# The token mixing's residual: by transposes of the DMA queue and adds of VectorE in PSUM, in place of matmuls with the identity

## The chip, the cores and the metric

The kernel runs on one core of one Trainium2 chip. The metric is device time in microseconds (us); a run of the kernel is one execution, and the time of a kernel is the median of its runs. The profile is of one execution.

## The reference, cut to what matters

Three blocks follow each other for each of 4 batches of 576 tokens: an attention that keeps only scores near the row's maximum, an MLP mixer (token mixing, then channel mixing, both with a residual), and a gated feed-forward with a convolution of three taps over the tokens. The change lies in the token mixing, whose result with its residual is `u`.

```python
# attention, per head
scores = where(scores >= max(scores) - tau, scores, -1e9); attn = softmax(scores); x = attn @ v
# mixer
h  = maximum(xt @ w_tok1, 0) @ w_tok2          # xt: x with channels ahead of tokens, 576 -> 256 -> 576
u  = x + h.transpose(0, 2, 1)                  # the residual in question
x2 = u + maximum(u @ w_ch1, 0) @ w_ch2         # 512 -> 1536 -> 512
# gated feed-forward
f  = maximum(x2 @ w_in, 0); gate = sigmoid(conv3(f)); out = (f * gate) @ w_out
```

## The kernel before, in words

Every large product is made of three float16 products: each operand is split into a high part and a low part (`_h`, `_l`), and high*high, high*low and low*high are added in one PSUM tile.

**Attention.** `attention(b)` walks through 36 slots of a batch: four pairs of heads, nine slots each. A slot has 128 queries: scores on PE (L308 or L312), row maximum on DVE (L324), exponential on ACT (L336), masking on DVE (L343), the split into two halves on ACT (L348) and POOL (L352), a transpose by the DMA queue of SP (L357, `pt<-ph`, nine blocks of 128x128), and some slots later the product with V on PE (L367, L370). `norm` divides by the row sum and splits the result x into `xp`: `xh` on ACT (L395), `xl` on POOL (L396), with tokens on the partitions: four blocks of 128 tokens, and a fifth with the last 64 tokens.

**Token mixing.** `tok(b, p)` runs once for each pair of heads p of each batch b. Its first step makes the hidden layer (L407) and splits it into `rh`, `rl`. Its two further steps make `u` for one stretch of tokens each (256 and 320, `SPL`): matmuls with `w_tok2` (L422) accumulate in one PSUM bank `up`, and between them PE adds the residual to the same bank: for each block of 128 tokens and for `xh` and `xl` one matmul that has the block as its weights and the identity (scaled by 1/`UDS`) as its moving operand (L427), which transposes the block and adds it. Then ACT writes the high part of `u` from the bank (L429), DVE the low part from the bank and the high part (L430), and the bank is free.

**Dense stages.** `dense(b)` follows for the whole batch: L547 (512 to 1536), L565 (1536 to 512), L598 with the convolution and the gate (`gate`: L581 on ACT, L583 twice on DVE, L585 on ACT, L586 on DVE, L587 on ACT, L588 on POOL, for each of eight row blocks f) and L621/L624 (the output product, which needs the gates of all f).

**What sets the order.** The attention of batch b+1, and its `tok`, is woven into `dense(b)` by counting steps. So the token mixing of batch 2 runs beside `dense(1)`, and that of batch 3 beside `dense(2)`: in each the first two pairs of heads fall into the stages of L565 and early L598, the third into the middle of the gates, the fourth behind the output product, right ahead of the next `dense`. A scheduler sets the final order of each engine from priorities and its own estimate of times; on the chip each engine then goes through its list strictly in order.

**Banks.** PSUM has eight banks. While attention and dense work run together, four are held by scores (two slots), one by the product with V, and three (4, 5, 6) go round between the dense tiles and `tok` (`dbank`, `free`): a bank is handed out in the order in which banks came free in the program, and PE waits if its last reader has not finished. In `dense(3)` banks 0 to 3 join them. All buffers with the tag "x" (the attention's tiles, the gate's `ct`, loads) come from one pool of 15.

Of the kernel before, what the change touches and what calls it, by code (L numbers as in the profile page):

```python
# [9 lines left out]
F16 = mybir.dt.float16  # L10
I32 = mybir.dt.int32
U16 = mybir.dt.uint16
AF = mybir.ActivationFunctionType
ALU = mybir.AluOpType
# [5 lines left out]
def kernel(ctx: ExitStack, tc: tile.TileContext, q, k, v, tau,  # L20
# [7 lines left out]
    nc = tc.nc  # L28
    B, NPR, _, S = q.shape
    H, D = 2 * NPR, 64  # L30
    P = 128
# [7 lines left out]
    NS = S // P  # L39
    R0 = NS * P  # L40
    SPL = [(0, 256), (256, S - 256)]
    NB32 = 2
# [10 lines left out]
    UDS = 1.0 / (WS * WS2)  # L53
# [6 lines left out]
    qk2 = ctx.enter_context(tc.tile_pool(name="qk2", bufs=2))  # L60
# [5 lines left out]
    V, A, G, T = nc.vector, nc.scalar, nc.gpsimd, nc.tensor  # L66
# [23 lines left out]
    for x, (sc, left) in enumerate(((0.125, 1.0), (QK, ESC))):  # L90
        V.tensor_scalar(out=qsc[:, x:x + 1], in0=tau_t, scalar1=0.0, scalar2=sc, op0=ALU.is_ge, op1=ALU.mult)
        V.scalar_tensor_tensor(out=mtaus[:, x:x + 1], in0=tau_t, scalar=-1.0 / left, in1=every,
                               op0=ALU.mult, op1=ALU.min)
# [198 lines left out]
    def dbank():  # L292

        x = free.pop(0)
        return x
# [102 lines left out]
    def tok(b, p):  # L398

        u, xp = u_t[b % 2][p], pair[b, p]["xp"]  # L400
        bk = dbank()
        rp = ps[:, bk]
        for t in range(NT):
            o = t * P
            for i, (wx, xx) in enumerate(((0, 0), (1, 0), (0, 1))):
                for j in range(NS + 1):
                    T.matmul(rp[:, o:o + P], wt1[wx][:, j, o:o + P], xp[xx][:, j],  # L407
                             start=(i == 0 and j == 0), stop=(i == 2 and j == NS))
        rh = p2.tile([P, NT, P], F16, tag="rh", name="rh")
        rl = p2.tile([P, NT, P], F16, tag="rl", name="rl")  # L410
        r3 = rp[:, :TK].rearrange("p (t c) -> p t c", t=NT)
        A.activation(out=rh, in_=r3, func=AF.Relu)
        V.scalar_tensor_tensor(out=rl, in0=r3, scalar=0.0, in1=rh, op0=ALU.max, op1=ALU.subtract)
        free.append(bk)
        yield
        rr = (rh, rl)
        for s0, n in SPL:
            bk = dbank()
            up = ps[:, bk]
            for i, (rx, wx) in enumerate(((0, 0), (1, 0), (0, 1))):  # L420
                for t in range(NT):
                    T.matmul(up[:, :n], rr[rx][:, t], wt2[wx][:, t, s0:s0 + n],  # L422
                             start=(i == 0 and t == 0), stop=(i == 2 and t == NT - 1))
                for j in range(NS + 1):
                    if i < 2 and s0 <= j * P < s0 + n:
                        m = P if j < NS else S - R0
                        T.matmul(up[:, j * P - s0:j * P - s0 + m], xp[i][:, j], ident if j < NS else ident2,  # L427
                                 start=False, stop=False)
            A.activation(out=u[0][:, s0:s0 + n], in_=up[:, :n], func=AF.Copy, scale=UDS)  # L429
            V.scalar_tensor_tensor(out=u[1][:, s0:s0 + n], in0=up[:, :n], scalar=UDS,  # L430
                                   in1=u[0][:, s0:s0 + n], op0=ALU.mult, op1=ALU.subtract)
            free.append(bk)
            if s0 == 0:
                yield
        del pair[b, p]
        yield
# [14 lines left out]
    def attention(b):  # L451
# [9 lines left out]
        for i in range(c0, c1, NSL):  # L461
            bb, p, _ = where(i + NSL)
            if bb < B:
                start(i - 1, prep(bb, p), (1, 2, 2, 1, 1, 1))
            start(i + NSL - 1 + lag + 2, tok(b, where(i)[1]), (2, 1, 1))
# [194 lines left out]
    for b in range(B):  # L660
        att = attention(b + 1) if b + 1 < B else iter(())
        n = 0
# [65 lines left out]
```

## Time and profile before

| what | value |
|---|---|
| time, three runs | 793.1, 795.9, 797.14 us; median 795.9 us |
| the profiled execution | 798.93 us, of which 797.1 us are the span from its first to its last instruction |
| PE busy | 742.8 us, 93% of the span |
| DVE, ACT, POOL busy | 495.5, 471.0, 421.8 us |
| matmuls with the identity (L427) | 160, of which 80 in batches 2 and 3 |

Busy time is the union of an engine's instructions. A matmul's duration in the profile runs from its start to the modelled end of its results, so two that follow each other overlap; what a matmul costs in a dense stream is the distance from start to start. "Idle before, releaser" says how long an engine stood idle and whose end let it go on.

### The profile page before, as it was taken

The numbers are of one execution on the slowest core, as the hardware profiler recorded it, in microseconds if no ns is written. First come the engines' busy times: TensorE is split into PE (matmuls) and PEld (weight loads), VectorE is DVE, ScalarE is ACT, GpSimd is POOL, SyncE is SP. The second block draws the span as 40 slices with busy tenths as digits, with TensorE's granted clock in tenths as the row PEclk, the third lists the DMA queues.
The fourth block names the chain that finished last, engine by engine and source line by source line (L and its number), as shares of the span: only waits on it lengthen the run. The fifth ranks groups of instructions, "written<-read, shape, count | busy, mean of one in ns | idle before, by whom it ended". The sixth has DMA issues, their size and how long they took to land. (4 is left out here: it accounts for less than half of the span.)

```text
span 797.1 us, 18473 instructions
## 1 busy us (share of the span) xinstructions
PE 742.8 (93%) x7388; PEld 562.1 (71%) x7388; DVE 495.5 (62%) x837; ACT 471.0 (59%) x998; POOL 421.8 (53%) x471
## 2 busy tenths in 40 slices
PE   5579979898998889999999999999999999999998
PEld 3457657676776675678878875788887856887764
DVE  5568877786767683367677892566876960322370
ACT  6768876775766674466566862566565751220371
POOL 5977788877687572155555771265664840000040
PEclk9889989999999999999999999999999999999999
DMA  9989998888789640368676531667664401000001
GB/s 280 195 186 173 166 240 198 187 226 192 200 219 198 106 76 28 93 135 164 135 164 131 117 54 40 139 134 156 143 133 80 76 18 58 1 1 1 2 1 60
DMA packets 195047, 97.84 MB, mean 123 GB/s; under 512 B 174096, under 2 KB 176656, under 8 KB 194960
## 3 DMA queue, kind: packets, MB, share of 16 engines
q1 hardware_dynamic: 194640, 96.39, 55.0%
q8 instruction: 58, 0.95, 0.5%
q10 hardware_dynamic: 320, 0.26, 0.1%
q14 instruction: 29, 0.24, 0.1%
HBM read 42.36 MB, written 4.72 MB: 59 GB/s over the span
## 5 line engine op out<-in xcount | busy, mean ns | idle before, releaser
L352 POOL TENSOR_TENSOR ph<-e,ph 128x576 f16<-128x576 f32 x108 | 141.2, 1308 | 98.0 <-ACT ph L348 93.0
L565 PE MATMUL ps<-act_t,wc_h 128*128 128x256 f16 (+1 forms) x768 | 148.8, 286 | 0.0
L324 DVE TENSOR_REDUCE nm<-ps 128x1 f32<-128x576 f32 x144 | 108.3, 753 | 54.2 <-PE ps L312 27.0
L308 PE MATMUL ps<-kt,qt 128*128 128x288 f32 (+1 forms) x320 | 95.1, 458 | 27.5 <-DVE act_t L343 12.1
L588 POOL TENSOR_TENSOR act_t<-ct,act_t 128x576 f16<-128x576 f32 x32 | 46.6, 1455 | 138.8 <-ACT act_t L587 135.9
L547 PE MATMUL ps<-u_h,wc_h 128*128 128x256 f16 (+1 forms) x384 | 110.0, 287 | 2.0 <-DVE act_t L522 2.0
L547 PE MATMUL ps<-u_h,wc_l 128*128 128x256 f16 (+1 forms) x384 | 109.9, 287 | 0.0
L565 PE MATMUL ps<-act_t,wc_l 128*128 128x256 f16 (+1 forms) x384 | 109.7, 286 | 0.0
L547 PE MATMUL ps<-u_l,wc_h 128*128 128x256 f16 (+1 forms) x384 | 109.4, 287 | 0.0
L343 DVE SCALAR_TENSOR_TENSOR e<-ps,thr,e 128x576 f32<-128x576 f32 x108 | 87.7, 812 | 22.3 <-ACT e L336 9.8
L547 PEld LDWEIGHTS <-wc_h 128*128 128x128 f16 x768 | 75.4, 98 | 20.3 <-issue 1.3
L565 PEld LDWEIGHTS <-wc_h 128*128 128x128 f16 x768 | 75.0, 98 | 18.9 <-issue 0.5
L308 PEld LDWEIGHTS ps<-kt,qt 128*128 128x128 f32 (+1 forms) x320 | 54.1, 197 | 46.2 <-DVE act_t L343 16.5
L367 PE MATMUL ps<-vh,pt 128*128 128x65 f16 (+1 forms) x1080 | 72.1, 195 | 7.4 <-DMA pt<-ph 7.2
L621 PE MATMUL ps<-wo_h,act_t 128*128 128x512 f16 x256 | 76.3, 379 | 1.8 <-DVE u_l L430 1.3
L583 DVE SCALAR_TENSOR_TENSOR ct<-h,cw,ct 128x576 f32<-128x576 f32 x64 | 68.3, 1068 | 15.2 <-ACT ct L581 14.6
L598 PE MATMUL ps<-u_h,wi_h 128*128 128x256 f16 (+1 forms) x256 | 73.0, 286 | 4.3 <-DVE u_l L430 3.2
L367 PEld LDWEIGHTS <-pt 128*128 128x128 f16 (+1 forms) x1080 | 62.7, 101 | 19.3 <-DMA pt<-ph 10.7
L348 ACT ACTIVATE ph<-e 128x576 f16<-128x576 f32 x108 | 73.0, 676 | 2.1 <-DVE e L343 2.1
L598 PE MATMUL ps<-u_h,wi_l 128*128 128x256 f16 (+1 forms) x256 | 73.0, 286 | 0.0
L598 PE MATMUL ps<-u_l,wi_h 128*128 128x256 f16 (+1 forms) x256 | 73.0, 286 | 0.0
L621 PEld LDWEIGHTS <-act_t 128*128 128x128 f16 x384 | 36.7, 98 | 44.0 <-issue 2.1
(113 smaller groups left out, 1621.3 us busy)
## 6 DMA issues: line engine op xcount, KB each, us to landing
st<-in_moe_w_ch_dram SPq DMA_DIRECT2D x24, 512.0 KB, 4.2
ld<-in_v_dram SPq DMA_DIRECT2D x32, 288.0 KB, 3.4
kt<-ks SPq DMA_DIRECT2D x32, 144.0 KB, 2.7
st<-in_moe_w_in_dram SPq DMA_DIRECT2D x8, 512.0 KB, 4.2
st<-in_moe_w_out_dram SPq DMA_DIRECT2D x8, 512.0 KB, 5.2
out_dram<-ot SPq DMA_DIRECT2D x16, 256.0 KB, 2.0
qt<-in_q_dram SPq DMA_DIRECT2D x8, 288.0 KB, 3.9
kt<-in_k_dram SPq DMA_DIRECT2D x16, 144.0 KB, 3.8
```

The costliest lines, as they stand in the source:

```text
L308: T.matmul(s3[o:o + m, a], f32(st["qt"])[:, q0:q0 + m], f32(st["kt"][hh])[:, a * hn:(a + 1) * hn], start=True, stop=True)
L324: crit["max"] = V.tensor_reduce(out=nm, in_=c["s3"], axis=AX.XY, op=ALU.max, negate=True)
L343: crit["mask"] = V.scalar_tensor_tensor(out=e3, in0=c["s3"], scalar=c["thr"], in1=e3, op0=ALU.is_ge, op1=ALU.mult)
L348: A.activation(out=c["ph"][:, 0:S], in_=c["e"], func=AF.Copy)
L352: G.tensor_tensor(out=c["ph"][:, S:], in0=c["e"], in1=c["ph"][:, 0:S], op=ALU.subtract)
L367: T.matmul(dst[o:o + m], pt[:, j, o:o + m], vh[:, hh, j, 0:D + 1], start=(j == 0), stop=(j == NSL - 1))
L547: T.matmul(t, wc1[wx][:, f, c], u[c][ux][:, sl], start=(c == 0 and i == 0), stop=(c == NC - 1 and i == 2))
L565: T.matmul(t, wc2[wx][:, c, f], r_t(f, rx)[:, sl], start=(by_dve(c) and f == 0 and i == 0), stop=(f == NF - 1 and i == 2))
L583: V.scalar_tensor_tensor(out=ct, in0=ht[:, kk:kk + S], scalar=cw[:, kk, f:f + 1], in1=ct, op0=ALU.mult, op1=ALU.add)
L588: G.tensor_tensor(out=g_t(f, 1), in0=ct, in1=g_t(f, 0), op=ALU.subtract)
L598: T.matmul(t, wi[wx][:, f, c], u[c][ux][:, s0:s0 + n], start=(c == 0 and i == 0), stop=(c == NC - 1 and i == 2))
L621: T.matmul(t, g_t(f, gx)[:, j * P:(j + 1) * P], wo[wx][:, f], **lim)
```

## The change

For batches 2 and 3 (`b >= NB32`) the residual of the 512 first tokens no longer goes through PE. At the start of `tok` a tile `xt` is taken from the "x" pool, POOL clears its last 64 columns, and SP's queue issues two transposes (high and low half, four blocks of 128x128 each). PE leaves out the matmuls with the identity except those of the last 64 tokens. Once PE has finished a stretch, DVE scales the bank, adds the transposed high half and writes the sum back to the bank, then adds the low half in the bank. ACT and DVE then split it as before, without the scale. Batches 0 and 1 are as before.

```diff
     def tok(b, p):
         u, xp = u_t[b % 2][p], pair[b, p]["xp"]
+        xt = None
+        if b >= NB32:
+
+            xt = qk2.tile([P, 2, S], F16, tag="x", name="xt", bufs=15)
+            G.memset(xt[:, :, R0:S], 0.0)
+            for i in range(2):
+                nc.sync.dma_start_transpose(out=xt[:, i, 0:R0].rearrange("p (j t) -> p j t", t=P),
+                                            in_=xp[i][:, 0:NS].rearrange("p j c -> p (j c)"))
         bk = dbank()
...
                 for j in range(NS + 1):
-                    if i < 2 and s0 <= j * P < s0 + n:
+                    if i < 2 and s0 <= j * P < s0 + n and (j == NS or xt is None):
                         m = P if j < NS else S - R0
                         T.matmul(up[:, j * P - s0:j * P - s0 + m], xp[i][:, j], ident if j < NS else ident2,
                                  start=False, stop=False)
-            A.activation(out=u[0][:, s0:s0 + n], in_=up[:, :n], func=AF.Copy, scale=UDS)
-            V.scalar_tensor_tensor(out=u[1][:, s0:s0 + n], in0=up[:, :n], scalar=UDS,
-                                   in1=u[0][:, s0:s0 + n], op0=ALU.mult, op1=ALU.subtract)
+            sl, up = slice(s0, s0 + n), up[:, :n]
+            if xt is not None:
+                V.scalar_tensor_tensor(out=up, in0=up, scalar=UDS, in1=xt[:, 0, sl], op0=ALU.mult, op1=ALU.add)
+                V.tensor_tensor(out=up, in0=up, in1=xt[:, 1, sl], op=ALU.add)
+            uds = UDS if xt is None else 1.0
+            A.activation(out=u[0][:, sl], in_=up, func=AF.Copy, scale=uds)
+            V.scalar_tensor_tensor(out=u[1][:, sl], in0=up, scalar=uds, in1=u[0][:, sl],
+                                   op0=ALU.mult, op1=ALU.subtract)
             free.append(bk)
```

In the new file L407 is the transposes, L430 the matmuls with `w_tok2`, L435 the matmuls with the identity, L439 and L440 the two adds, L442 and L443 the split; the lines behind `tok` are 13 further down (L583 is L596, L586 is L599).

PE's list in the fourth pair of batch 3, the stretch of 256 tokens, before:

```order
L422 LDWEIGHTS rh
L422 MATMUL ps<-wt_h,rh 128x256
L427 LDWEIGHTS xh
L427 MATMUL ps<-ident,xh 128x128
L427 LDWEIGHTS xh
L427 MATMUL ps<-ident,xh 128x128
L422 LDWEIGHTS rl
L422 MATMUL ps<-wt_h,rl 128x256
```

The same place of the new program:

```order
L430 LDWEIGHTS rh
L430 MATMUL ps<-wt_h,rh 128x256
L430 LDWEIGHTS rl
L430 MATMUL ps<-wt_h,rl 128x256
L430 LDWEIGHTS rl
L430 MATMUL ps<-wt_h,rl 128x256
```

The two matmuls of `xh` between the products of `rh` and `rl` are gone, as are the two of `xl` behind those of `rl`.

DVE's list in the third pair of batch 3, in the middle of the gates (`ct` is the gate's tile, `u_2_l` the low part of the third pair's u), before:

```order
L586 SCALAR_TENSOR_TENSOR ct<-ct,h_147 128x576
L583 SCALAR_TENSOR_TENSOR ct<-h_148,cw,ct 128x576
L430 SCALAR_TENSOR_TENSOR u_2_l<-ps,u_2_h 128x256
L583 SCALAR_TENSOR_TENSOR ct<-h_148,cw,ct 128x576
L383 TENSOR_SCALAR rc<-ps 128x5
L384 RECIPROCAL rc<-rc 128x5
L387 TENSOR_TENSOR x_9357<-ps,rc 128x4x64
L390 SCALAR_TENSOR_TENSOR x_9357<-ps,rc,blk 128x128
L583 SCALAR_TENSOR_TENSOR ct<-h_147,cw,ct 128x576
L586 SCALAR_TENSOR_TENSOR ct<-ct,h_148 128x576
L430 SCALAR_TENSOR_TENSOR u_2_l<-ps,u_2_h 128x320
L583 SCALAR_TENSOR_TENSOR ct<-h_147,cw,ct 128x576
```

The same place of the new program, up to the low part of the first stretch and a little further:

```order
L599 SCALAR_TENSOR_TENSOR ct<-ct,h_147 128x576
L439 SCALAR_TENSOR_TENSOR ps<-ps,xt 128x256
L440 TENSOR_TENSOR ps<-ps,xt 128x256
L596 SCALAR_TENSOR_TENSOR ct<-h_148,cw,ct 128x576
L443 SCALAR_TENSOR_TENSOR u_2_l<-ps,u_2_h 128x256
L596 SCALAR_TENSOR_TENSOR ct<-h_148,cw,ct 128x576
L383 TENSOR_SCALAR rc<-ps 128x5
L384 RECIPROCAL rc<-rc 128x5
L439 SCALAR_TENSOR_TENSOR ps<-ps,xt 128x320
L387 TENSOR_TENSOR x_9357<-ps,rc 128x4x64
L596 SCALAR_TENSOR_TENSOR ct<-h_147,cw,ct 128x576
```

The two adds of the first stretch now stand between the gates of two row blocks, ahead of the next L583 (L596). Of the second stretch, L439 stands among the steps of `norm`, L440 behind L390, and the low part two places behind the L586 (L599) of `h_148`, with an L583 (L596) between them.

## Rows read from the trace of the kernel before

**Rows 1.** The page: PE's busy time, and the clock granted in 40 slices.

```profile
PE 742.8 (93%) x7388; PEld 562.1 (71%) x7388; DVE 495.5 (62%) x837; ACT 471.0 (59%) x998; POOL 421.8 (53%) x471
...
PEclk9889989999999999999999999999999999999999
```

**Rows 2.** Busy times by stage: stretch, length, PE, PEld, DVE, ACT, POOL, clock, DMA.

```profile
437.00:484.00 47.00, 44.76 (x508) 33.96 (x506) 40.27 (x54) 34.64 (x73) 31.55 (x31) 1.00 0.39 77
484.00:503.00 19.00, 19.00 (x157) 11.32 (x156) 0.48 (x2) 3.65 (x9) 1.64 (x2) 1.00 0.20 72
503.00:609.00 106.00, 106.00 (x1182) 86.33 (x1180) 76.03 (x133) 65.48 (x144) 57.66 (x76) 1.00 0.66 136
609.00:657.00 48.00, 46.15 (x512) 34.62 (x511) 36.25 (x51) 33.60 (x70) 29.82 (x27) 1.00 0.29 51
```

**Rows 3.** Timeline of PE in the fourth pair of batch 3: start, us, instructions.

```profile
674.82 0.28 PE L427 MATMUL ps<-ident,xh 128*128 128x128 f16 x2
674.93 0.38 PE L422 MATMUL ps<-wt_h,rl 128*128 128x256 f16 x2
675.15 0.28 PE L427 MATMUL ps<-ident,xl 128*128 128x128 f16 x2
```

**Rows 4.** Groups of DVE by shape, 380 to 680: count, busy us, mean ns, idle before.

```profile
L583 DVE SCALAR_TENSOR_TENSOR ct<-h,cw,ct 128x576 f32<-128x576 f32 x32 | 36.3, 1134 | 3.8 <-ACT ct L581 3.5
...
L532 DVE TENSOR_TENSOR u_l<-us,u_h 128x320 f16<-128x320 f32 x6 | 6.7, 1122 | 0.1
...
L430 DVE SCALAR_TENSOR_TENSOR u_l<-ps,u_h 128x320 f16<-128x320 f32 x8 | 3.9, 485 | 1.5 <-ACT u_h L429 1.5
...
L430 DVE SCALAR_TENSOR_TENSOR u_l<-ps,u_h 128x256 f16<-128x256 f32 x8 | 3.3, 418 | 27.9 <-ACT u_h L429 27.9
```

**Rows 5.** The group of the whole span that writes PSUM from DVE.

```profile
L157 DVE SCALAR_TENSOR_TENSOR ps<-st,ps 128x512 int32<-128x512 int32 x42 | 29.1, 693 | 21.7 <-ACT ps L156 7.3 <-POOL ph L352 6.0 <-issue 5.3
```

**Rows 6.** Waits of PE between 380 and 680: us in total, times, longest.

```profile
PE ps L598 <- DVE u_l L430: 1.4, 1, 1.4
PE ps L598 <- ACT h L574: 1.0, 1, 1.0
...
PE ps L621 <- DVE u_l L430: 0.6, 2, 0.3
PE ps L621 <- ACT act_t L587: 0.3, 1, 0.3
PE ps L621 <- POOL act_t L588: 0.3, 1, 0.3
```

**Rows 7.** Timeline of DVE among the gates of `dense(2)`, third pair of batch 3.

```profile
638.40 1.00 DVE L586 SCALAR_TENSOR_TENSOR ct<-ct,h 128x576 f32<-128x576 f32 x1 [0.75 <-ACT ct L585]
641.09 1.00 DVE L583 SCALAR_TENSOR_TENSOR ct<-h,cw,ct 128x576 f32<-128x576 f32 x1 [1.69 <-ACT ct L581]
...
647.91 1.01 DVE L586 SCALAR_TENSOR_TENSOR ct<-ct,h 128x576 f32<-128x576 f32 x1 [0.75 <-ACT ct L585]
649.11 2.57 DVE L583 SCALAR_TENSOR_TENSOR ct<-h,cw,ct 128x576 f32<-128x576 f32 x2 [0.19 <-ACT ct L581]
652.42 0.76 DVE L586 SCALAR_TENSOR_TENSOR ct<-ct,h 128x576 f32<-128x576 f32 x1 [0.75 <-ACT ct L585]
```

**Rows 8.** SP's transposes of the attention: issue ns, and time to landing.

```profile
L357 SPq DMA_TRANSPOSE pt<-ph x108: 1242/1302/2678, 108.5 to 637.1; - x108
...
DMA to landing us min/median/max: 3.2/3.4/7.4
```

**Rows 9.** Timeline of POOL, second pair of batch 2: the low half of x.

```profile
421.20 0.67 POOL L396 TENSOR_TENSOR xl<-x,xh 128x256 f16<-128x256 f32 x1
```

**Rows 10.** Timeline of ACT, the same pair: the first evacuation of u.

```profile
432.36 0.38 ACT L429 ACTIVATE u_h<-ps 128x256 f16<-128x256 f32 x1 [0.28 <-PE ps L422]
```

**Rows 11.** Timeline of DVE at the seam to `dense(2)`, fourth pair of batch 2.

```profile
502.94 0.42 DVE L430 SCALAR_TENSOR_TENSOR u_l<-ps,u_h 128x256 f16<-128x256 f32 x1 [13.69 <-ACT u_h L429]
```

**Rows 12.** Timeline of PE there: the next use of that bank.

```profile
504.59 0.27 PE L547 MATMUL ps<-u_h,wc_h 128*128 128x256 f16 x1
```

## The prediction

> **What bounds the kernel now.** I read the page first, then the stages, then the waits of PE inside them. PE is busy for 742.8 of 797.1 us, and its granted clock is at the full level from slice 14 on [rows 1]; what it loses, it loses in the first 300 us, which the change does not touch. By stages [rows 2] PE is busy for all 106 us of 503 to 609 and all 19 us of 484 to 503, but for 44.8 of 47 us in 437 to 484 and 46.2 of 48 us in 609 to 657. These two are the stages of the gates, beside which the third pairs of batches 2 and 3 fall, and there DVE is the busiest engine after PE: 40.3 of 47 us and 36.3 of 48 us. The waits name what PE stood for: 1.4 + 0.6 us for L430 (a bank of PSUM that the token mixing still held), 1.0 us for the gate's L574, 0.3 + 0.3 us for the last gate (L587, L588) [rows 6]. So PE sets the pace nearly everywhere, and in the gates' stages DVE's list does, through banks and through the last gate. A matmul less on PE is worth its distance to the next one; an instruction more on DVE costs nothing until it makes a bank or a gate late.
>
> **What is removed.** Each `tok` loses eight matmuls of 128x128 (four blocks, two halves), so 8 x 8 = 64. Two of them start at 674.82 and the next matmul at 674.93 [rows 3]: 0.055 us each, their weight loads hidden. 64 x 0.055 = 3.5 us, or 0.44 us a pair of heads. The Trainium skill (TensorE: Matmul & The Clock Gate, Back-to-back issue gap) gives 81 ns as the sustained spacing of a 128-column matmul that has its own weight load; by it the saving would be 5.2 us. This trace shows 55 ns, and the sum goes by that.
>
> **What is added on DVE.** Two instructions a stretch. Before has none with a PSUM input, a float16 tile from SBUF and a PSUM output. Nearest below is L430, which has those inputs and writes SBUF: 418 ns for 256 columns, 485 for 320 [rows 4]; L157 does write PSUM, 693 ns for 512 [rows 5], which is where L430's two points lead (about 1.05 ns for each further column: 485 + 192 x 1.05 = 687). Above is L532, with all operands in SBUF: 1122 ns for 320 [rows 4]. I take L430: two adds cost 0.84 us for 256 columns and 0.97 us for 320, 14.5 us over the 16 stretches; at the upper end they would be up to 2.2 us a stretch. The skill (SBUF — State Buffer, Who interferes with whom) says that DVE with two SBUF inputs contends with a GpSimd instruction that reads SBUF and with at most one it doesn't. L583, which has two, averages 1134 ns for 576 columns [rows 4], twice what L430's slope leads to; the trace agrees, and the adds have one.
>
> **What is added in queues.** Sixteen transposes on SP of four blocks, against nine of the attention's, which take 1.30 us to issue and land 3.2 to 7.4 us later, 3.4 in the median [rows 8]; four blocks by that ratio issue in about 0.6 us (an estimate). They need `xl`; in the second pair of batch 2, the closest, it is done at 421.87, and the first evacuation starts at 432.36 [rows 9, 10], 10.5 us later. New on the list of SP is that they stand behind some of the attention's transposes, whose lead over their matmuls is several slots, and delay the loads behind them by 1.2 us, which nothing on PE waits for at once. I put this at 0; if a landing takes 7.4 us and SP is two transposes late, the cover is gone, and DVE stands at L439 for up to 2 us with row maxima and gates queued behind it. The memset on POOL (128 columns) and the "x" buffer that `xt` holds: 0, since POOL has 15 us or more free in each gates' stage [rows 2]; a late buffer would show as a late exponential.
>
> **What moves.** A bank is now held from PE's end over L439, L440, L442, L443 instead of over two steps: 0.84 or 0.97 us longer, plus DVE's queue.
>
> - *First, second and fourth pairs* (six). DVE has room or the next user of the bank is 1 us or more behind, so PE keeps its 0.44 us: -2.6 us. One exception is the seam to `dense(2)`: DVE ends L430 at 503.36 and the bank's next user starts at 504.59, 1.2 us later [rows 11, 12]. The new list of DVE has both stretches' adds ahead of the first low part: L439 can start where the evacuation on ACT started, 0.4 us ahead of 502.94; with 0.84, 0.97 and 0.42 us behind it, and a little for the second stretch's matmuls, the low part ends at 504.7 to 504.8. PE, with half of its 0.44 us less between the two, is there at about 504.4. +0.3 us. At the last seam the four more banks cover it.
> - *Third pairs* (two). Here PE gets nothing, since it waits for the last gate anyway [rows 6], and DVE's list decides. In batch 3 [rows 7] the new list puts the first two adds into the idle 1.69 us ahead of 641.09: free. From there I place the new list with the durations of the old one (each starting 0.08 us ahead of the end of the one before, as the rows do): both remaining adds, 0.80 us, are paid until the low part, and the following L586 starts 0.4 us later than its 647.91. The pair of L583 behind it waited 0.19 us for ACT, so the last L586 (652.42) is 0.2 us late. In batch 2 the new list moves three steps of `norm` ahead of the last gate as well, 2.3 us in all with the four adds, against about 2 us of idle gaps behind ACT that they fall into: 0.3 to 0.7, I take 0.5. Together +0.7 us.
>
> **Sum**: -2.6 + 0.3 + 0.7 = -1.6 us: from 798.9 us for the profiled execution to 797.3. Its own time is 3.0 us above the median of the three runs, 795.9; from there 794.3 us. That is 0.2% less. About 0.5% (4 us) is what a measurement of this kernel can tell from no change; its three runs lie that far apart.
>
> **The rivals.**
> - *PE-bound throughout: the adds are free.* The new list of PE puts more work between the third pairs' stretches and the next use of their banks (in batch 2, by the program's order, 29 matmuls of 320 columns in place of 12 behind the first stretch; behind the second 16 of 512 columns and 24 others in place of 6 and 12). Then all 3.5 us are kept and the 2.0 us of waits for L430 [rows 6] vanish: -5.5 us, 790.4. Against it: the idle time of DVE in the gates' stages is nearly all behind ACT within one gate, so it isn't free to be filled everywhere.
> - *The other side: DVE is the bound of the gates' stages.* If the adds cost what L532 does, or each delays a contended L583, a third pair costs up to 2 x 2.2 us on DVE, and PE, which waits for the last gate, pays it: 2 x 4.4 us less the 2.6 us of the other pairs, +6 us, 802. It decides from about 1.7 us of unhidden time a stretch of the two third pairs (4 x 1.7 - 2.6 = 4). For it: DVE's busy share there; against: L430's steady durations.
> - *The transposes are late.* A first pair's transposes follow two of the attention's closely; DVE then stands at L439 and PE's banks with it, 1 us in each of the eight pairs: +6 us, 802.
> - *The scheduler's other order* shifts PE's waits by 1 us here and there, with either sign; that is in the range of each case.
>
> **Chances.** The forecast (within 0.5%: 792 to 798): 0.55. The free adds: 0.26, nearly all of it faster by over 0.5%. DVE-bound 0.12, transposes late 0.07: slower. The range 790.3 to 799.5 takes in the free adds and the lower edge of the slower ones; the likeliest case alone is 792.5 to 797.
>
> **What would show it.** In the new profile: 80 - 64 = 16 matmuls of L435 in batches 2 and 3, and PE's busy time down by some 3.5 us; L439 and L440 near 0.42 and 0.485 us, steady beside POOL. Right if PE's waits for L443 stay near 2 us in all and those for L600 and L601 (the last gate) rise by under 1 us; the free adds if they sink towards 0; DVE-bound if those for L443, L600, L601 or L343 sum to 8 us and more. Idle time of DVE at L439 behind a DMA `xt` would show late transposes. I would be wrong above all in how much of the adds falls into DVE's gaps, which I placed by hand in one stage and only weighed in the other.

## The result, and the profile after

The changed kernel takes 804.9 us (median of four runs, 802.9 to 806.6); the kernel before, run beside it, 796.5 us (793.1 to 800.3). The ratio is 1.0104, 95% interval 1.0065 to 1.0143: about 8 us slower. The forecast was 794.3 us with a range of 790.3 to 799.5; the time lies outside.

The profiled execution took 803.7 us, with a span of 801.9 us. The part ahead of `dense(1)`, which the change doesn't touch, differs between executions (over the profiles of all runs, `dense(1)` starts between 320.9 and 333.6 us), so the two traces are compared from a fixed place: the first matmul of a dense stage. The rows of L547 (before) and L560 (after) with their first and last start, for `dense(1)` and `dense(2)`, before:

```profile
L547 PE MATMUL ps<-u_h,wc_h x96: 272/290/301, 330.8 to 376.7; 128*128 128x256 f16 x48, 128*128 128x320 f16 x48
L547 PE MATMUL ps<-u_h,wc_h x96: 272/290/301, 503.4 to 549.4; 128*128 128x256 f16 x48, 128*128 128x320 f16 x48
```

and after:

```profile
L560 PE MATMUL ps<-u_h,wc_h x96: 272/290/301, 329.1 to 375.0; 128*128 128x256 f16 x48, 128*128 128x320 f16 x48
L560 PE MATMUL ps<-u_h,wc_h x96: 270/290/300, 508.5 to 554.7; 128*128 128x256 f16 x48, 128*128 128x320 f16 x48
```

From the one to the other `dense(1)` lasted 503.4 - 330.8 = 172.6 us, now 508.5 - 329.1 = 179.4 us: +6.8 us. From there to PE's last matmul it is 290.2 us before and 289.9 us now. The whole loss lies in `dense(1)`, beside which batch 2's token mixing runs; batch 3's costs nothing on balance (beside it the removed matmuls alone give 2.0 us, and the adds alone take 1.9: E3 and E2 below). Within `dense(1)` it lies in the gates: from their first matmul to the first of the output product 40.3 us before and 49.5 us after.

The gates' stage in the new kernel (columns as in [rows 2]: stretch, sum, busy time of PE, its weight loads, DVE, ACT and POOL, granted clock, DMA share, GB/s):

```profile
437.00:484.00 47.00, 39.92 (x448) 31.00 (x445) 37.74 (x57) 33.93 (x71) 32.52 (x34) 0.93 0.47 92
```

In 437 to 484, PE is busy for 39.9 us against 44.8 [rows 2], and DVE, which should have more to do, for less as well: 37.7 against 40.3. Neither is the bound there any more. What PE waited for, from 380 to 680 (columns: engine and line, what it waited for, us in total, times, longest):

```profile
PE ps L367 <- DVE x L387: 2.4, 1, 2.4
PE ps L430 <- ACT h L587: 1.6, 1, 1.6
PE ps L611 <- ACT h L587: 1.6, 2, 1.1
PE ps L367 <- DMA pt<-ph: 1.5, 2, 1.4
PE ps L312 <- DVE e L343: 0.8, 2, 0.7
PE ps L634 <- DVE u_l L443: 0.6, 1, 0.6
PE ps L634 <- ACT h L587: 0.6, 1, 0.6
PE ps L560 <- DVE u_l L443: 0.3, 1, 0.3
```

Half of this is for the attention, and not for the token mixing's banks as in [rows 6]: L367 is the product with V, which waits for `norm` (L387) and for `pt`, the transposed probabilities, and L312 the scores. Together they are 4.7 us, where the kernel before has only

```profile
PE ps L312 <- DVE e L343: 0.6, 1, 0.6
```

These waits stand at 448 to 460 us, near the end of batch 2's attention. (The 3.8 us for L587, ACT's evacuation of the gate's `h`, come later: 2.3 us of them at 474 and 482 us, the rest in `dense(2)`. That they follow from the attention's delay is not shown.) Around the attention's waits the granted clock falls (columns: stretch, sum, busy time of PE, granted clock, DMA share, GB/s):

```profile
447.00:450.00 3.00, 1.02 (x14) 1.00 0.70 140
450.00:452.00 2.00, 1.39 (x27) 0.55 1.00 233
452.00:454.00 2.00, 2.00 (x21) 0.59 0.36 139
454.00:456.00 2.00, 2.00 (x19) 1.00 0.00 0
458.00:460.00 2.00, 0.64 (x5) 1.00 0.68 132
460.00:462.00 2.00, 2.00 (x32) 0.61 0.54 105
462.00:464.00 2.00, 2.00 (x10) 0.53 0.23 42
464.00:466.00 2.00, 2.00 (x34) 1.00 0.56 108
```

Twice PE has hardly worked and then runs for some 4 us near its lower level (1.2 GHz). Against full clock that is, as an estimate from these rows, 1.39 x 0.45 + 2 x 0.41 + 2 x 0.39 + 2 x 0.47 = 3.2 us. The waits in this stage sum to 7.1 us against 2.2 us before, 4.9 more; with the 3.2 us of the clock, less 1.8 us for the removed matmuls of four pairs, that gives 6.3 of the 6.8 us.

SP's list shows where the delay enters. Its transfers around the first pair's transposes, before (columns: start, length, engine and line, transfer, count):

```profile
394.09 0.53 SPq L248 DMA_DIRECT2D ld<-in_q_dram  x1
394.73 0.40 SPq L249 DMA_DIRECT2D ld<-in_k_dram  x1
```

and after:

```profile
389.60 2.80 SPq L357 DMA_TRANSPOSE pt<-ph  x2
392.49 1.23 SPq L407 DMA_TRANSPOSE xt<-xh  x1
393.78 1.26 SPq L407 DMA_TRANSPOSE xt<-xl  x1
395.13 0.53 SPq L248 DMA_DIRECT2D ld<-in_q_dram  x1
395.71 0.42 SPq L249 DMA_DIRECT2D ld<-in_k_dram  x1
```

The `pt` transposes ahead start 1.6 us earlier than before, and so does `dense(1)` itself (329.1 against 330.8 us). Then two `xt` hold the queue for 1.25 us each, and the load of the next heads' q starts 1.0 us later than before: 2.6 us lost in one place. At the second pair it happens again (q's load at 429.7 us against 426.8). Counted from the first matmul of `dense(1)`, the two loads are 2.7 and 4.6 us late, and the `pt` that PE waits for near 460 us (456.6 against 452.5 us) is 5.8 us late.

The scores of the heads that these loads are for are not what is held up. Behind the first pair's transposes come the batch's last heads; their `kt` has landed 12 us ahead of its first score in the kernel before and still 11 us ahead in the new one. Behind the second pair's come the first heads of batch 3. What the loads hold up is ACT, which goes through its list in order: the split of the new q (L226) waits for the load, and an exponential of the running attention (L336) stands behind the split. At the first pair, before:

```profile
397.24 0.78 ACT L226 ACTIVATE qs<-ld,qsc 128x576 f16<-128x576 f32 x1 [0.83 <-DMA ld<-in_q_dram]
397.92 0.72 ACT L336 ACTIVATE e<-ps,bias 128x576 f32<-128x576 f32 x1
```

and after:

```profile
398.27 0.78 ACT L226 ACTIVATE qs<-ld,qsc 128x576 f16<-128x576 f32 x1
398.95 0.72 ACT L336 ACTIVATE e<-ps,bias 128x576 f32<-128x576 f32 x1
```

Counted from the first matmul of `dense(1)`, the exponential starts 2.7 us later, and at the second pair 4.6 us later (433.66 against 430.78 us). ACT stood for these two loads before already, 0.83 and 2.07 us, so nothing covers a later one; the masking, `ph` and `pt` of the slot come behind the exponential.

### The profile page after: what moved, and what is told of

It is laid out like the page before. It is cut to its first block, busy times and chain, and to the rows that moved or that the text cites. A ratio compares the mean times of both kernels' runs of the same rounds, so it can differ in the third digit from the quotient of the medians.

```text
span 801.9 us, 18424 instructions
## 1 busy us (share of the span) xinstructions
PE 743.0 (93%) x7324; PEld 559.7 (70%) x7324; DVE 502.2 (63%) x869; ACT 470.7 (59%) x998; POOL 421.4 (53%) x479
## 5 line engine op out<-in xcount | busy, mean ns | idle before, releaser
L601 POOL TENSOR_TENSOR act_t<-ct,act_t 128x576 f16<-128x576 f32 x32 | 44.8, 1402 | 136.8 <-ACT act_t L600 135.3
L560 PE MATMUL ps<-u_h,wc_h 128*128 128x256 f16 (+1 forms) x384 | 109.7, 287 | 2.0 <-DVE act_t L535 1.5
L560 PE MATMUL ps<-u_h,wc_l 128*128 128x256 f16 (+1 forms) x384 | 109.6, 286 | 0.0
L560 PE MATMUL ps<-u_l,wc_h 128*128 128x256 f16 (+1 forms) x384 | 108.8, 286 | 0.0
L343 DVE SCALAR_TENSOR_TENSOR e<-ps,thr,e 128x576 f32<-128x576 f32 x108 | 87.7, 812 | 18.3 <-ACT e L336 8.8
L560 PEld LDWEIGHTS <-wc_h 128*128 128x128 f16 x768 | 75.2, 98 | 20.1 <-issue 1.1
L367 PE MATMUL ps<-vh,pt 128*128 128x65 f16 (+1 forms) x1080 | 75.0, 198 | 12.2 <-DMA pt<-ph 9.6
L308 PEld LDWEIGHTS ps<-kt,qt 128*128 128x128 f32 (+1 forms) x320 | 53.7, 196 | 45.6 <-DVE act_t L343 16.7
L367 PEld LDWEIGHTS <-pt 128*128 128x128 f16 (+1 forms) x1080 | 64.4, 103 | 22.3 <-DMA pt<-ph 14.1
L611 PE MATMUL ps<-u_h,wi_h 128*128 128x256 f16 (+1 forms) x256 | 74.7, 292 | 2.1 <-ACT h L587 1.6
L596 DVE SCALAR_TENSOR_TENSOR ct<-h,cw,ct 128x576 f32<-128x576 f32 x64 | 68.5, 1071 | 12.5 <-ACT ct L594 11.9
L535 DVE SCALAR_TENSOR_TENSOR act_t<-ps,act_t 128x256 f16<-128x256 f32 (+1 forms) x96 | 43.0, 455 | 39.0 <-ACT act_t L534 38.3
```

The source lines that it names most:

```text
L308: T.matmul(s3[o:o + m, a], f32(st["qt"])[:, q0:q0 + m], f32(st["kt"][hh])[:, a * hn:(a + 1) * hn], start=True, stop=True)
L343: crit["mask"] = V.scalar_tensor_tensor(out=e3, in0=c["s3"], scalar=c["thr"], in1=e3, op0=ALU.is_ge, op1=ALU.mult)
L367: T.matmul(dst[o:o + m], pt[:, j, o:o + m], vh[:, hh, j, 0:D + 1], start=(j == 0), stop=(j == NSL - 1))
L560: T.matmul(t, wc1[wx][:, f, c], u[c][ux][:, sl], start=(c == 0 and i == 0), stop=(c == NC - 1 and i == 2))
L596: V.scalar_tensor_tensor(out=ct, in0=ht[:, kk:kk + S], scalar=cw[:, kk, f:f + 1], in1=ct, op0=ALU.mult, op1=ALU.add)
L601: G.tensor_tensor(out=g_t(f, 1), in0=ct, in1=g_t(f, 0), op=ALU.subtract)
```

## The experiments

A table at their end holds the main ones. "`dense(1)`" is the time between the two first matmuls as above. Three profiled kernels in which PE's list in `dense(1)` is the same (the kernel before, E4 and E8) show 172.6, 172.8 and 173.0 us, so about half a microsecond can be read there from one profile where the lists are the same, which the times can't tell. The theories were A (the transposes on SP's queue), B (the adds on DVE) and C (the 64 matmuls had covered the attention's chain).

**E1, the transposes alone.** An excerpt of its difference from the changed kernel:

```diff
-                    if i < 2 and s0 <= j * P < s0 + n and (j == NS or xt is None):
+                    if i < 2 and s0 <= j * P < s0 + n:
...
-            if xt is not None:
-                V.scalar_tensor_tensor(out=up, in0=up, scalar=UDS, in1=xt[:, 0, sl], op0=ALU.mult, op1=ALU.add)
-                V.tensor_tensor(out=up, in0=up, in1=xt[:, 1, sl], op=ALU.add)
-            uds = UDS if xt is None else 1.0
+            uds = UDS
```

> The sixteen transposes into xt stay, xt is read by nobody, PE adds the whole residual as before and DVE has no adds: the output is the reference's. Theory A (the transposes are the loss: SP's queue is 2.5 us longer a pair, and with it the scores of the next heads fall behind the dense matmuls in PE's list): slower than before by 5 to 11 us, since nothing is saved on PE, with PE standing in the gates of dense(1) as in the changed kernel (its waits there 5 us or more). Theory B (the adds on DVE are the loss): within 1 us of before. Theory C (the 64 matmuls were cover for the attention's chain, and PE stands in their place): within 1 us of before.

Measured: +1.0% (interval 0.65 to 1.36), `dense(1)` 179.9 us. The transposes that nobody reads cost all that the change costs. The exponentials behind the two splits of q start 2.5 and 5.8 us later than before, counted from `dense(1)`. PE's waits from 375 to 500 us:

```profile
PE ps L367 <- DMA pt<-ph: 4.4, 3, 2.9
PE ps L367 <- DVE x L387: 2.1, 1, 2.1
PE ps L631 <- DVE u_l L440: 0.9, 1, 0.9
```

**E2, the adds alone.** An excerpt of its difference from the changed kernel (the transposes are out as well, and PE adds the whole residual):

```diff
+    zt = const.tile([P, 320], F16, name="zt")
+    G.memset(zt, 0.0)
...
-                V.scalar_tensor_tensor(out=up, in0=up, scalar=UDS, in1=xt[:, 0, sl], op0=ALU.mult, op1=ALU.add)
-                V.tensor_tensor(out=up, in0=up, in1=xt[:, 1, sl], op=ALU.add)
+                V.scalar_tensor_tensor(out=up, in0=up, scalar=UDS, in1=zt[:, :n], op0=ALU.mult, op1=ALU.add)
+                V.tensor_tensor(out=up, in0=up, in1=zt[:, :n], op=ALU.add)
```

> No transposes; PE adds the whole residual as before, and DVE's two adds a stretch add a constant tile of zeros, so the output is the reference's. Theory A: 0 to 2 us slower than before, from the third pairs. Theory B: slower by 6 us or more. Theory C: as A.

Measured: +0.73% (0.49 to 0.98), `dense(1)` 178.0 us. Theory A had 0 to 2 us and failed here: the adds alone cost nearly as much as the transposes alone, and the two together no more than one. But the waits are again the attention's (`pt` 3.8 us in all, the longest 2.9), not the gates', as DVE as the bound would show.

**E3, the removal alone** (neither adds nor transposes).

> The 64 matmuls are gone and nothing takes their place: the residual of the first 512 tokens of batches 2 and 3 is left out. Theory A and theory B: faster than before by 2.5 to 3.5 us (0.3 to 0.45%). Theory C: within 1 us of before or slower, PE waiting in the gates of dense(1).

Measured: -0.24% (-0.44 to -0.05), `dense(1)` 171.9 us, from its start to the end 2.7 us less. Theory C falls: PE's saving is real, about as priced.

**E4, the last batch alone** (`b > NB32` in place of `b >= NB32`).

> The change in the last batch alone; batch 2 is as before, and so is PE's list up to the last batch's attention. Theory A, as the traces of before and after place the loss (+6.6 us up to 484 us, -1.1 us from there to the end): as fast as before or up to 2 us faster, 0 to -0.25%. Theory B: half of the loss stays, slower by 3 to 5 us. Theory C: as A.

Measured: -0.1% (-0.35 to +0.17), `dense(1)` 172.8 us, and 289.8 us from there. As the traces said, the loss is batch 2's.

**E5 and E6, PE's list held fast.** Ahead of scores that it takes to be late, the scheduler may move dense matmuls that are ready. In the changed kernel it did: batch 2's attention has forty groups of scores (four matmuls each), and between the 22nd and the 23rd of them PE's list has 4.0 groups of twelve dense matmuls, where before it has 2.3; it pays at the end, with 2.0 between the third last and the last, where before it has 4.0. So I made a pair of kernels in which each step of `dense(1)` is queued on PE behind the scores that stand ahead of it in the text:

```diff
-                    T.matmul(s3[o:o + m, a], st["qt"][:, hh, q0:q0 + m],
+                    crit["score"] = T.matmul(s3[o:o + m, a], st["qt"][:, hh, q0:q0 + m],
...
-        for i, _ in enumerate(dense(b)):
+        for i, _ in enumerate(steps(dense(b), ("score",)) if b == 1 else dense(b)):
```

With it, scores and dense matmuls of `dense(1)` alternate in both kernels in the same way. The rule holds only these two: the places of the products with V and of the token mixing's matmuls, and the lists of ACT, DVE and POOL, may still differ. E5 is the kernel before with the rule, E6 the changed one.

> The kernel before, with one rule for PE's list: each step of dense(1) is queued on PE behind the scores that stand ahead of it in the program's text, so that no dense matmul can be moved ahead of scores that the scheduler thinks late. PE's list moves by at most 2 groups of 12 dense matmuls in dense(1) and is the same elsewhere. Theory A1 (it is PE's list that loses the time, not the queue's delay on the chip): 0 to 2 us either side of before. Theory A2 (the queue's delay on the chip): the same; this run is the base of the next.

> The changed kernel with the same rule: in dense(1) the dense matmuls and the scores then stand in PE's list exactly as in the pinned kernel before, while transposes, adds and the removal are all there. Theory A1: 0 to 3 us faster than the pinned kernel before (794 to 797), the gates of dense(1) from 49.4 back to 41 or 42 us. Theory A2: as slow as the changed kernel, 5 us or more over the pinned kernel before, with PE now standing at the scores. Theory B (DVE's added work): slower than the pinned kernel before by 4 us or more, DVE behind in the gates.

Measured: E5 +0.41% (0.17 to 0.65), `dense(1)` 173.6 us; E6 +0.76% (0.44 to 1.07), `dense(1)` 177.8 us. Between the two lie 4.2 us in `dense(1)`; without the rule it was 6.8. So the order of scores and dense matmuls took some 2.6 us of the loss, and most of it is left when that order is the same. Neither A1 nor A2 had that; both parts are there. PE's waits in E5, from 375 to 500 us:

```profile
PE ps L621 <- DVE u_l L430: 1.4, 1, 1.4
PE ps L367 <- DMA pt<-ph: 1.1, 1, 1.1
PE ps L598 <- DVE u_l L430: 0.5, 1, 0.5
```

and in E6:

```profile
PE ps L312 <- DVE e L343: 3.2, 3, 2.5
PE ps L367 <- DMA pt<-ph: 1.9, 2, 1.7
PE ps L634 <- ACT h L587: 1.1, 1, 1.1
PE ps L367 <- DVE x L390: 0.8, 1, 0.8
```

The dense matmuls no longer run ahead, and PE stands at the scores (L312) instead: the attention's chain itself is late.

**E7, adds and removal, no transposes** (E2's tile of zeros in the changed kernel).

> The changed kernel without the transposes: DVE adds a constant tile of zeros instead of xt, so the residual of the first 512 tokens of batches 2 and 3 is left out. The adds alone cost 5.8 us, the removal alone gave 1.9 us. If the adds cost by DVE's time (B): 802 or more, 3 to 6 us over before. If they cost through the order that they led the scheduler to (A1): anything from -2 to +6 us, decided by whether the gates of dense(1) take 40 to 42 us or 47 us and more in the profile.

Measured: +0.1% (-0.15 to +0.36), `dense(1)` 175.5 us, from there 2.0 us less than before. The gates took 45.6 us, between the two cases that the expectation names.

**E8, tile and memset alone** (E1 without the loop of the transposes).

> The kernel before with xt taken from the pool of 15 buffers and its last columns cleared by POOL, without transposes and adds: the output is the reference's. PE's list is the same as before. Theory that the buffer taken from the attention's pool is the loss: slower by 2 us or more. All others: within 1 us of before.

Measured: +0.1% (-0.24 to +0.42), `dense(1)` 173.0 us. The buffer from the attention's pool costs nothing.

**E9 and E10, transposes and adds apart, PE's list held fast** (E1 and E2 with the rule of E5).

> The transposes alone (xt is read by nobody, PE adds the whole residual), under the rule of the pinned kernels; PE's list in dense(1) stands as in both of them. Between the pinned pair, dense(1) up to its output product took 4.9 us longer with the change (1.8 us in the stage ahead of the gates, 3.3 us in the gates, less 0.2), and its list was the same. If the delay of SP's queue makes it: the gates 3 us and more over the pinned kernel before (44 us and more). If the adds make it: 41 to 42 us.

> The adds alone (of a constant tile of zeros, PE adds the whole residual), under the same rule. If the delay of SP's queue makes the 4.9 us: the gates of dense(1) at 41 to 42 us. If the adds make it: 44 us and more. If both are needed together: both runs at 42 to 43 us.

Measured: E9 +0.69% (0.35 to 1.03), `dense(1)` 177.9 us, 4.3 over E5. E10 +0.40% (0.1 to 0.71), `dense(1)` 174.1 us, 0.5 over E5. With scores and dense matmuls in the same order, the adds cost 0.5 us in `dense(1)`; the other 4.9 us of E2 were the order that they led the scheduler to. E2's trace shows most of it, on POOL: the two low halves of `norm` (L398) stand ahead of the last slot's `ph` (L354),

```profile
461.31 2.15 POOL L398 TENSOR_TENSOR xl<-x,xh 128x256 f16<-128x256 f32 x2
463.42 1.27 POOL L354 TENSOR_TENSOR ph<-e,ph 128x576 f16<-128x576 f32 x1
```

where the kernel before has `ph` first, as E10 has:

```profile
465.01 1.28 POOL L352 TENSOR_TENSOR ph<-e,ph 128x576 f16<-128x576 f32 x1
...
467.00 0.67 POOL L396 TENSOR_TENSOR xl<-x,xh 128x256 f16<-128x256 f32 x1
```

Counted from `dense(1)`, that `ph` ends 2.7 us later; PE waits 2.9 us for its `pt`, and the granted clock is at half for the 3.4 us behind.

The transposes delay the chip also where the order of scores and dense matmuls stands: against E5, the exponentials behind the two splits of q start 2.1 and 3.2 us later in E9, and 0.0 and 0.3 in E10. But E9's 4.3 us are not shown to be the queue's alone. Its lists of ACT, DVE and POOL stand in another order than E5's in many places (at 391.6 us ACT has the next slot's L329 ahead of an exponential that E5 has ahead of it, and which starts 1.7 us later for it); those of E10 hardly differ from E5's. PE's waits in E9, from 375 to 500 us:

```profile
PE ps L312 <- DVE e L343: 2.5, 2, 1.9
PE ps L608 <- ACT h L584: 1.7, 2, 1.6
PE ps L367 <- DMA pt<-ph: 1.4, 1, 1.4
PE ps L608 <- DVE u_l L440: 0.5, 1, 0.5
```

**E11 and E12, the change only where PE doesn't wait**: the fourth pairs alone (`b >= NB32 and p == 3`), and with them the first two pairs of the last batch.

> The change in the fourth pairs of batches 2 and 3 alone, which run beside the output products, where the attention is over and SP's queue empty. By the stages of the changed kernel, which gained 1.0 us in the output product of dense(1) and 2.0 us from that of dense(2) to the end: 1.5 to 3 us faster than before (0.2 to 0.4%), the gates of dense(1) as before. If the adds hold the bank at the seam to dense(2) for longer than PE saves: within 0.5 us of before.

> The change in the fourth pair of batch 2 and in the first, second and fourth of batch 3: the pairs beside stages where PE never waits. If the first two pairs of batch 3 bring their 0.44 us each and leave the gates of dense(2) alone: 0.5 to 1 us faster than the fourth pairs alone. If their transposes make the end of the attention late as in dense(1): slower than the fourth pairs alone by 1 us or more, in the gates of dense(2).

Measured: E11 -0.19% (-0.44 to +0.06), E12 -0.13% (-0.44 to +0.17); from the start of `dense(1)` to the end E11 took 0.3 us more than before, E12 1.6 us less. Neither can be told from no change, and the 1.5 to 3 us expected of E11 are not in its profile.

**E13 and E14, the queue's time or its place, PE's list held fast.** E13 is E9 with one transpose a pair (`range(1)`); E14 is E9 with both asked for in the second step, so that on SP they stand behind the next heads' loads and `qt` and ahead of `kt`:

```diff
         yield
+        if xt is not None:
+            xt = qk2.tile([P, 2, S], F16, tag="x", name="xt", bufs=15)
...
         rr = (rh, rl)
```

> As the transposes alone under the pinned rule, but only that of the high half: one a pair in place of two. Two cost 1.3 us ahead of the gates of dense(1) and 3.4 us in them, at the same list of PE. If the cost is the time that they hold SP's queue (2.5 us a pair, now 1.25): about half, the gates at 42.4 to 43.4 us and 0.4 to 0.9 us ahead of them. If what counts is that anything stands there at all, or a fixed event such as an order among transposes and other transfers: 44 us and more.

> Two transposes a pair again, but asked for in the second step of the token mixing: on SP they stand behind the next heads' loads of q and k and their qt, and ahead of kt, in place of ahead of the loads. If it is the delay of the loads that counts (they start the next heads' scores): the gates at 41 to 42.5 us. If it is the queue's time wherever it falls (kt and the attention's transposes behind them are as late): 44 us and more.

Measured: E13 +0.27% (-0.03 to +0.57), `dense(1)` 174.5 us, 0.9 over E5. E14 +0.27% (0.01 to 0.52), `dense(1)` 174.0 us, 0.4 over E5. Two transposes ahead of the loads cost 4.3 us, one 0.9, two behind the loads 0.4. So it is not the queue's time wherever it falls, and not in proportion: of two transposes ahead of the loads the first costs 0.9 us and the second 3.4. The exponentials behind the two splits of q start 2.1 and 3.2 us later than in E5 with two transposes, 1.1 and 2.5 with one, 0.0 and 0.9 with two behind the loads. This rests on one profile each, and the lists of ACT, DVE and POOL differ here too; by the times, none of the three can be told from E5 (1.0069, 1.0027 and 1.0027 of before, against 1.0041, each to 0.3%).

**E15 and E16, one transpose for both halves**, without and with the rule of E5. `xh` and `xl` lie side by side in one tile `xm`:

```diff
-            xt = qk2.tile([P, 2, S], F16, tag="x", name="xt", bufs=15)
-            G.memset(xt[:, :, R0:S], 0.0)
-            for i in range(2):
-                nc.sync.dma_start_transpose(out=xt[:, i, 0:R0].rearrange("p (j t) -> p j t", t=P),
-                                            in_=xp[i][:, 0:NS].rearrange("p j c -> p (j c)"))
+            xt = qk2.tile([P, 2 * S], F16, tag="x", name="xt", bufs=15)
+            nc.sync.dma_start_transpose(out=xt[:, 0:2 * R0].rearrange("p (j t) -> p j t", t=P),
+                                        in_=xm.rearrange("p x j c -> p (x j c)"))
...
+                if k < n:
+                    V.tensor_scalar(out=up[:, k:], in0=up[:, k:], scalar1=UDS, scalar2=None, op0=ALU.mult)
```

> The whole change with one transpose a pair for both halves (xh and xl side by side in one tile, eight blocks), the last 64 columns scaled by an instruction of their own on DVE, no memset: the output is the reference's. If a transpose's time on SP is per instruction (1.25 us for four blocks as for nine): SP loses 1.3 us a pair, not 2.5, and the kernel is 2 to 4 us faster than the changed one: 0.5% (0.1 to 0.8) over before. If it is per block here: as the changed kernel, +1%.

> The same with the pinned list of PE in dense(1). If the queue's time decides: the gates of dense(1) at 42.4 to 43.4 us as with one transpose, about 2 us less than in the pinned changed kernel, 0 to +0.4% against before. If not: 44.5 us as there.

Measured: E15 +0.27% (0.03 to 0.51), `dense(1)` 177.9 us; E16 -0.18% (-0.35 to -0.01), `dense(1)` 173.9 us, 0.3 over E5. A transpose of eight blocks holds SP as long as one of four (E16):

```profile
L409 SPq DMA_TRANSPOSE xt<-xm x8: 1232/1308/2199, 392.8 to 653.6; - x8
```

**E17 and E18, what the runs seemed to point to**: E16 with the transpose one slot later, behind the loads, and in E18 the rule in `dense(2)` as well.

```diff
-            start(i + NSL - 1 + lag + 2, tok(b, where(i)[1]), (2, 1, 1))
+            start(i + NSL - 1 + lag + 2, tok(b, where(i)[1]), (2, 1, 1) if b < NB32 else (1, 1, 1, 1))
...
         yield
+        if xt is not None:
+            xt = qk2.tile([P, 2 * S], F16, tag="x", name="xt", bufs=15)
...
+            yield
         rr = (rh, rl)
```

> The whole change as the runs before suggest it: one transpose a pair for both halves, asked for one slot after the first step of the token mixing, so that on SP it stands behind the loads of the next heads, and PE's list pinned in dense(1). If the place ahead of the loads is what cost: the gates of dense(1) at 41 to 42 us and nothing ahead of them, 1 us less than with one transpose ahead of the loads; 0.2 to 0.5% faster than before. If the queue's time counts wherever it falls: as e16, -0.2%.

> The same, with PE's list pinned in dense(2) as well, whose gates took 41.9 us in e16 against 38.6 before. If the scheduler's order made these 3.2 us: the gates of dense(2) at 39 to 40 us and 1 to 2 us faster than e17, 0.3 to 0.7% faster than before. If DVE's adds make them: as e17 or slower by the cost of the rule itself, 1 us.

Measured: E17 +0.87% (0.53 to 1.22), `dense(1)` 178.4 us; E18 +1.04% (0.64 to 1.44). Both expectations failed. PE's waits in E17, from 375 to 500 us:

```profile
PE ps L367 <- DMA pt<-ph: 3.7, 4, 2.9
PE ps L619 <- DVE u_l L451: 3.4, 1, 3.4
```

The transpose of the third pair now lands at 472.9 us, 3.0 us later than in E16, and the adds of both its stretches stand behind it on DVE (L445 at 473.5 and 473.9 us), among gates. The bank that PE filled at 468.3 to 469.1 us gets its low part (L451) only at 477.8 us, and the next gate (L619) waits 3.4 us for it. E14 could not show this, since nobody read `xt` there. Why `pt` is waited for more as well (3.7 us against 1.3 in E16) wasn't settled.

The main runs:

| run | time against before (95% interval) | `dense(1)`, us | from there to the end, us |
|---|---|---|---|
| before | 1 | 172.6 | 290.2 |
| changed | 1.0104 (1.0065 to 1.0143) | 179.4 | 289.9 |
| E1 transposes | 1.0101 (1.0065 to 1.0136) | 179.9 | 290.7 |
| E2 adds | 1.0073 (1.0049 to 1.0098) | 178.0 | 292.1 |
| E3 removal | 0.9976 (0.9956 to 0.9995) | 171.9 | 288.2 |
| E5 before, list held | 1.0041 (1.0017 to 1.0065) | 173.6 | 290.1 |
| E6 changed, list held | 1.0076 (1.0044 to 1.0107) | 177.8 | 289.2 |
| E9 transposes, list held | 1.0069 (1.0035 to 1.0103) | 177.9 | 290.5 |
| E10 adds, list held | 1.0040 (1.0010 to 1.0071) | 174.1 | 292.1 |
| E13 one transpose, list held | 1.0027 (0.9997 to 1.0057) | 174.5 | 290.3 |
| E14 behind the loads, list held | 1.0027 (1.0001 to 1.0052) | 174.0 | 290.0 |
| E16 one for both, list held | 0.9982 (0.9965 to 0.9999) | 173.9 | 288.2 |
| E17 and one slot later | 1.0087 (1.0053 to 1.0122) | 178.4 | 289.9 |

One thing in it doesn't fit: E5's time is 0.41% over before, at least 1.4 us by its interval, and its profile from `dense(1)` on only 0.9 us (463.7 against 462.8). Measured against E5's own time, E9 costs 0.3% (2.2 us) where the profiles say 4.7. The sizes from the profiles are therefore good for comparing stages, and to some 2.5 us for the times.

## Why the prediction was wrong

**The step that failed is what is added in queues.** I put two transposes of four blocks at 0.6 us each by the ratio of blocks, 1.2 us a pair, "which nothing on PE waits for at once", and therefore at 0. They take 1.25 us each, 2.5 us a pair. "At once" was right of PE, and beside the point: the loads of q and k stand behind them, ACT waits for q with an exponential of the running attention behind the wait, and through `pt` the delay reaches PE 50 us later. It grows from pair to pair (2.7 and 4.6 us at the loads, 5.8 at the `pt`). With scores and dense matmuls held in their order, the transposes cost 4.3 us (E9 over E5), behind the loads 0.4 (E14); how much of the 4.3 is the order of the other engines' lists is open. I looked for the cover in the `pt` transposes' lead and didn't ask what was next on the list, q and k, and what ACT had behind them.

**The adds were put too low as well**, at 0.3 + 0.7 = 1.0 us. E10 against E5 shows 0.5 us in `dense(1)` and 2.0 us from there on (292.1 against 290.1), though in `dense(2)` no order was held.

**The scheduler's order was a rival of 1 us "here and there".** It is 2.6 us in the changed kernel, and 4.9 us for the adds alone (E2 over before, against E10 over E5). The lists I compared were right; I read DVE's third pairs and PE's fourth in them, and not how many dense matmuls stand between scores in `dense(1)`, where 2.3 groups had become 4.0.

**"PE sets the pace nearly everywhere"** held for the profile, and hid that batch 2's attention in `dense(1)` had hardly any slack: the scores waited 0.6 us for L343 there before already. A wait that long didn't tell how near the chain was; ACT's waits of 0.83 and 2.07 us for the loads did.

Right were the durations: the adds took what L430's rows led to, 0.43 and 0.49 us against 0.42 and 0.485 [rows 4]:

```profile
L440 DVE TENSOR_TENSOR ps<-ps,xt 128x320 f32<-128x320 f32 x7 | 3.4, 493 | 0.1
L439 DVE SCALAR_TENSOR_TENSOR ps<-ps,xt 128x320 f32<-128x320 f32 x7 | 3.4, 491 | 0.6 <-PE ps L430 0.6
L440 DVE TENSOR_TENSOR ps<-ps,xt 128x256 f32<-128x256 f32 x7 | 3.0, 430 | 2.6 <-DMA xt<-xl 2.5
L439 DVE SCALAR_TENSOR_TENSOR ps<-ps,xt 128x256 f32<-128x256 f32 x7 | 3.0, 430 | 19.2 <-PE ps L430 19.2
```

The removal is worth 2.7 us from `dense(1)` on (E3) against 3.5 us priced, and 1.9 us by the times. PE's busy time, which was to fall by 3.5 us, stayed at 743.0 us against 742.8: what the removed matmuls gave, the lower clock took back. One reading was off without consequence: L583's 1134 ns are 1.5 times the 754 ns to which L430's two points lead for 576 columns, not twice. (In the trace of the kernel before, the 18 of its 64 instructions that ran while POOL was idle took 802 to 819 ns; all that took over 900, up to 1926, ran beside POOL.) The seam to `dense(2)` was forecast at +0.3 us, and PE waits 0.3 us there for L443. The waits for L443 sum to 0.9 us and so stayed under 2. The late transposes had a rival with a chance of 0.07 and the right time, 802 us, but with another place: DVE standing at L439. DVE did wait for `xt`, 2.5 us in two places, as the third row shows; what decided is what the transposes make late, not that they are late.

**What stays open**: how much of E9's 4.3 us the lists of ACT, DVE and POOL make, which no run held; why E5's time is further from before than its profile; and whether the transposes on another queue than SP would spare the loads, which wasn't tried.

No version beats the kernel before by what a measurement can tell: E16 comes nearest, at -0.18% (-0.35 to -0.01).

## What to carry to other kernels

An instruction in a queue costs whatever stands behind it there: follow the transfers behind it to the engine that waits for them, then what stands behind that wait in the engine's own list, however many slots later it reaches the bound, and price it by a measured instruction, not by its bytes. Where latency-bound work is threaded through dense work, the cover is a number that can be read from the list, the dense matmuls between one link and the next; a change that leads the scheduler to spend it early shows up as a wait at the other end. To tell the order's share from the chip's, hold the order fast in both kernels and measure each part again; here only scores and dense matmuls were held, and the rest of the order is still in the numbers.

## What was unexpected of the hardware

- A transpose of the queue between buffers of SBUF took 1.25 us of SP's time for four blocks, 1.31 for eight (E16) and 1.30 for nine [rows 8]: the price is the instruction's, within these sizes.
- The clock's share. After the waits around 450 and 460 us the granted clock was at 0.53 to 0.61 for some 4 us each, 3.2 us in all; in E17 it was at 0.50 behind a wait of 3.4 us, but at 1.00 behind one of 2.9 us. In E6 a wait of 2.5 us at about the same place left it at 1.00, as did all of E5, E9, E10, E13, E14 and E16. So part of what the order cost in the changed kernel came through the clock: with scores and dense matmuls held, E6 waited as long in `dense(1)` as the changed kernel and kept it.
